# Batch 0 of an attention and feed-forward kernel: transposes back to back, sums a group later, even queries ahead of most feed-forward pieces

## The chip, the cores and the metric

The kernel runs on one core of a Trainium2 chip. A core has a matrix engine (PE, TensorE), VectorE (DVE), ScalarE (ACT), GpSimd (POOL) and SyncE (SP), which run beside each other and wait for one another through semaphores; each works through its own instructions in order. The metric is the device time of one execution in microseconds (us).

## What is computed

Inputs are q, k and v of 8 batches, 12 heads, 448 tokens and 64 numbers per head, and four weight matrices of 768 x 768. The output has 3584 rows of 768.

```
scores = scale * q @ k.T                        # per batch and head
e      = exp(scores - m)                        # m: row maximum
attn   = e / (sum(e) + exp(-m) + 1e-09)
x      = (attn @ v), heads side by side         # [8*448, 768]
h      = max(max(x @ w1, x @ w2), x @ w3)
out    = h @ w_out
```

## The kernel before, in words

Four heads make a group, so each batch has three groups and there are 24 in all. A group's work on PE is: transposing its keys and queries (`transpose_pe` L184 in two halves called pairs, `transpose_once` L214 for the whole group, from group 7 on by a DMA, L229); the scores (`scores` L282), keys times queries, which ACT turns into e by one exponential per score tile (L316) that reads PSUM; the sums (`av`, L524, made of `av_tail` L326 and `av_main` L345), e times the values with a column of ones, divided on DVE by three instructions (L363, L366, L369) into xn; and the transposition of xn into xT (`x_transpose_pe` L389, `x_transpose_all` L404), copied by DVE.

Feed-forward work is cut into pieces: `up_piece` (L427) makes 12 (or 6) matmuls of one weight matrix w[i], i being 0, 1 or 2, and DVE copies the result into hT (L445) or takes the maximum with it (L447); `out_piece` (L452) multiplies hT with w_out. Pieces stand in a list. `fill` (L507) takes pieces off its front while its credit of columns is positive, so PE gets a piece between attention steps. `STEP` (L522) is exactly one piece of two blocks of 192 columns. `share` (L604) spreads what is left over the visits until the next batch is added.

The time at issue is batch 0, groups 0 to 2, before the steady loop at L618. There each group is done in two parts: the odd query blocks "O" (192 columns) first, the even ones "E" (256 columns) later. L546 names the steps: `S01`, `S23` and `S46` are score units, two units to a tile for O and E; `("v", g, p)` is a sum of group g, pair p. The order is written by hand from L547 to L596. Two groups' e buffers exist (`e_buf`, L153).

PSUM comes from two rings: `ps_s` with three buffers (score tiles, sums, and transposes if asked) and `ps_b` with two (transposes, xT and feed-forward results). Asking for a buffer makes its first writer wait for the last reader of the use before. The engine that copies a transposed block out is an argument: DV is DVE, AC is ACT, PL is POOL. `shift_q` (L238) copies queries between partitions for the later groups, on POOL. `prep_v` (L376) puts the values into their buffers, on POOL or DVE.

All inputs are loaded by DMAs that POOL issues, in the order of the program (L142 to L151, then L528 to L533, L553 to L555 and L594 to L596), and converted to 16 bits on the way. A POOL copy that waits for a load, such as `prep_v(1, PL)` at L529, holds back the loads behind it. `warm` (L164) makes matmuls on zeros whose result nobody reads. `make_identity` (L145) makes the matrix that transposes use, on POOL.

Of the kernel before, what the change touches and what calls it, by code (L numbers as in the profile page):

```python
# [16 lines left out]
MMDT = FP16  # L17
# [4 lines left out]
def kernel(  # L22
# [11 lines left out]
    nc = tc.nc  # L34
# [13 lines left out]
    NE, NO = 4 * HP, 3 * HP  # L48
# [17 lines left out]
            name=nc.get_next_instruction_name(),  # L66
# [6 lines left out]
    cpool = ctx.enter_context(tc.tile_pool(name="const", bufs=1))  # L73
# [7 lines left out]
    ps_s = ctx.enter_context(tc.tile_pool(name="ps_s", bufs=3, space=bass.MemoryType.PSUM))  # L81
    ps_b = ctx.enter_context(tc.tile_pool(name="ps_b", bufs=2, space=bass.MemoryType.PSUM))
# [18 lines left out]
    def load_qk(i, names="kq", prs=(0, NP)):  # L101
        b, g = groups[i]
        tiles = raw.setdefault(i, {})
        for nm in names:
            if nm not in tiles:
                t = ld_bufs[nm][i % NL]
                if nm == "q" and i < NF:
                    nc.vector.memset(t[:, 0 : NP * T + 2 : NP * T + 1, :], 0.0)
                tiles[nm] = t
            src = {"q": q, "k": k}[nm][b].rearrange("h s d -> (h s) d")  # L110
            src = src.rearrange("(g r x t) d -> g x r (t d)", g=NG, r=NP, x=P)[g]
            p0, p1 = prs
            nc.gpsimd.dma_start(  # L113
                out=tiles[nm][:, 1 : NP * T + 1].rearrange("x (r t) d -> x r (t d)", r=NP)[:, p0:p1],
                in_=src[:, p0:p1],
            )
# [16 lines left out]
    def load_weight(i, gs=(0, 1, 2)):  # L133
        w = (moe_w1, moe_w2, moe_w3, moe_w_out)[i]
        src = w.rearrange("(g hf p) f -> g p hf f", g=3, hf=2)
        for g in gs:
            nc.gpsimd.dma_start(out=w_sb[i][:, 2 * g : 2 * g + 2, :], in_=src[g])  # L137


    wz = cpool.tile([128, 512], MMDT, name="wz")  # L140
    nc.vector.memset(wz, 0.0)
    load_qk(0, "kq", (0, 1))  # L142
    load_qk(0, "kq", (1, 2))
    ident16 = cpool.tile([128, 128], MMDT, name="ident16")
    make_identity(nc, ident16)  # L145
    load_qk(1, "kq", (0, 1))
    load_qk(1, "kq", (1, 2))
    load_v(0)
# [15 lines left out]
    def warm(n, cols=512):  # L164
        ps = ps_b.tile([128, 512], FP32, tag="b", name="warm")
        for _ in range(n):
            nc.tensor.matmul(
                out=ps[:, 0:cols], lhsT=wz[:, 0:128], rhs=wz[:, 0:cols], start=True, stop=True
            )
# [14 lines left out]
    def transpose_pe(i, pr, pool, k_eng, q_engs):  # L184


        def tile_of():
            if pool is ps_s:
                return ps_s.tile([128, 2, 1024], MMDT, tag="s", name="trT")[:, 0]
            return ps_b.tile([128, 1024], MMDT, tag="b", name="trT")  # L190

        kr, qr = raw[i]["k"], raw[i]["q"]
        kj = (0, 1, 2) if pr == 0 else (3, 4, 5, 6)
        qt = (-1, 1, 3, 5, 0, 2, 4) if pr == 0 else (6, 8, 10, 12, 7, 9, 11, 13)
        n = -(-len(qt) // len(q_engs))
        jobs = [(k_eng, "k", kj[0], kr, [2 * b for b in kj])]
        for e, eng in enumerate(q_engs):
            jobs.append((eng, "q", pr * 7 + e * n, qr, qt[e * n : (e + 1) * n]))
        if i not in KT:
            KT[i] = att_pool.tile([P, T * 128], MMDT, tag="KT", name="KT")  # L200
            QT[i] = att_pool.tile([P, (NB + 1) * 128], MMDT, tag="QT", name="QT")
        tps = [tile_of() for _ in jobs]
        for tp, (eng, nm, o, src, toks) in zip(tps, jobs):
            for j, t in enumerate(toks):
                nc.tensor.transpose(
                    out=tp[:, ts(j, 128)],
                    in_=src[:, t + 1 : t + 3, :].rearrange("x t d -> x (t d)"),
                    identity=ident16,
                )
        for tp, (eng, nm, o, src, toks) in zip(tps, jobs):  # L210
            dst = {"k": KT, "q": QT}[nm][i]
            evac(eng, dst[:, o * 128 : (o + len(toks)) * 128], tp[:, 0 : len(toks) * 128])
# [273 lines left out]
    def add_up(b, q0, qn, order):  # L486
        w = 1 if qn == S else 2
        for i, f0 in order:
            fcs = tuple(range(f0, f0 + w))
            pieces.append((up_piece, (b, fcs, i, q0, qn), NDC * w * (qn + 6)))  # L490
# [16 lines left out]
    def fill(cols):  # L507
        credit[0] += cols
        while pieces and credit[0] > 0:
            f, a, w = pieces.pop(0)  # L510
            f(*a)
            credit[0] -= w
        if not pieces:
            credit[0] = min(credit[0], 0.0)
# [10 lines left out]
        av_tail(i, ej, pr, PW[part])  # L525
        av_main(i, ej, pr, PW[part])

    load_weight(0, (0, 1))  # L528
    prep_v(1, PL)  # L529
    load_weight(0, (2,))  # L530
    prep_v(2, PL)
    load_qk(3)
    load_weight(1)  # L533
# [1 line left out]
    def attend(part, g, *steps):  # L535

        ej = (g + (part == "E") * NG) % NEB
        for st in steps:
            if st[0] == "s":
                for u in st[1:]:  # L540
                    scores(g, ej, u, part)
            else:
                pg, pr = st[1:]
                av(pg, pg % NEB, pr, "O")
# [3 lines left out]
    transpose_pe(0, 0, ps_s, DV, (AC, DV))  # L548
    transpose_pe(0, 1, ps_b, DV, (DV,))
    attend("O", 0, S01, S23, S46)  # L550
    warm(5)
    transpose_pe(1, 0, ps_b, AC, (DV,))
    load_qk(4)  # L553
    load_weight(2)
    load_v(3)  # L555
    attend("O", 1, S01)
    transpose_pe(1, 1, ps_b, AC, (DV,))
    attend("O", 1, S23, S46)
    prep_v(0, DV)
    attend("O", 1, ("v", 0, 0), ("v", 0, 1))  # L560
    transpose_pe(2, 0, ps_b, AC, (DV,))
    attend("O", 2, S01)
    transpose_pe(2, 1, ps_b, DV, (DV,))
    attend("O", 2, ("v", 1, 0), S23)
    x_transpose_pe(0, "O")
    attend("O", 2, S46, ("v", 1, 1), ("v", 2, 0))
    attend("E", 0, S01)
    x_transpose_pe(1, "O")
    attend("E", 0, ("v", 2, 1), S23)
    x_transpose_pe(2, "O")  # L570
    add_up(0, NE, NO, [(i, f) for i in range(3) for f in (0, 2, 4)])
    fill(STEP)
    attend("E", 0, S46)
    fill(STEP)

    for n in (4, 5):
        ej, part, g, pp, pg = n % NEB, "E", n - 3, "E", n - 4
        scores(g, ej, (0, 1), part)
        scores(g, ej, (2, 3), part)
        av(pg, 1 - ej, 0, pp)  # L580
        if n == 4:
            transpose_once(3, "q", AC)
        else:
            x_transpose_pe(0, "E")
        fill(STEP)
        scores(g, ej, (4, 5), part)
        scores(g, ej, (6,), part)
        av(pg, 1 - ej, 1, pp)
        if n == 4:
            transpose_once(3, "k", AC)  # L590
        fill(STEP)
        if n == 4:
            shift_q(3, PL)
            load_v(4)  # L594
            load_qk(5)
            load_weight(3)  # L596
# [21 lines left out]
    for i in range(3, NI):  # L618
        ej, pj = (i + 1) % NEB, i % NEB
        first = i == 3  # L620
        if PE_QK <= i + 2 < NI:
            transpose_dma(i + 2)
        if first:
            load_v(i + 2)
        for vi, units in enumerate(visits):
            n = 3 * i + vi
            scores(i, ej, units)
            if i == 4 and vi == 0:
                prep_v(i, DV)
            if vi < 2:  # L630
                av(i - 1, pj, vi, "E" if first else "EO")
            if vi == 1 and i > 3 * PE_X:
                x_transpose_dma(i - 1)
            if n in adds:
                add_batch(adds[n])
            per = STEP if first and vi < 2 else share(n)
            if vi == 0 and first:
                x_transpose_pe(1, "E")
            if vi == 2 and first:
                x_transpose_pe(i - 1, "E")  # L640
                fill(per / 2)
                prep_v(i, DV)
                add_up(0, 0, NE, [(w, f) for w in range(3) for f in (0, 2, 4)])
                add_out(0)
                per = share(n)
            if vi == 2 and 3 < i <= 3 * PE_X:
                x_transpose_all(i - 1)
            if first:
                fill(per)
                per = 0  # L650
            if i + 1 < PE_QK and vi < 2:
                transpose_once(i + 1, "qk"[vi], (AC, DV)[vi])
            fill(per)
        if i + 1 < PE_QK:
            shift_q(i + 1, nc.gpsimd)
        if first:
            load_qk(i + 3)
        if i < 5:
            load_more(i + 3, i + 4)
        if 5 <= i + 1 < NI:  # L660
            prep_v(i + 1, nc.gpsimd)
        if PE_QK <= i + 2 < NI:
            shift_q(i + 2, nc.gpsimd)
        if i >= 5:
            load_more(i + 3, i + 4)
# [37 lines left out]
```

## Time and profile before

| What | us |
|---|---|
| median of 5 runs (342.68 to 344.95) | 343.85 |
| the profiled execution's own time | 346.1 |
| its span, first to last instruction | 344.3 |
| PE busy | 331.0 |
| DVE busy | 187.0 |
| ACT busy | 151.4 |
| POOL busy | 148.4 |

The profile is of one execution. Busy time adds an engine's instructions up; matmuls overlap, so a busy PE is not one at its peak. The slices cut the span into 40 parts of 8.6 us and give busy shares in tenths. A row of the timeline has the start, the time to the end of the last of its instructions, the engine, line, operation, operands and number, and in brackets how long the engine stood before it and which instruction ended that wait. A row of a table of windows has the stretch, its length, then busy time and number of instructions of PE, PE's weight loads, DVE, ACT and POOL, then the granted clock of PE as a share of full speed, the mean busy share of the DMA engines, and GB/s.

### The profile page before, as it was taken

The page shows a single profiled execution, that of the slowest core. Times are in us where ns is not written, and L with a number is a line of the kernel's source. Part 1 is how long each engine was busy: PE and PEld are TensorE (multiplying, and loading weights), DVE is VectorE, ACT ScalarE, POOL GpSimd, SP SyncE. Part 2 cuts the span into 40 slices and gives each one's busy share as a digit, 9 for nine tenths or more (in the row PEclk, how much of TensorE's full clock was granted, in tenths as well). Part 3 has the DMA queues.
Part 4 walks back from the last instruction along what each step waited for, and adds up shares of the span by engine and source line. Part 5 has one row for each costly group of instructions (what it writes and reads, how often), then busy time and mean ns, then how long its engine had stood idle before and what let it go on. Part 6 is the DMA issues. An engine that isn't in the chain of part 4 may idle for free.

```text
span 344.3 us, 9827 instructions
## 1 busy us (share of the span) xinstructions
PE 331.0 (96%) x4175; PEld 200.4 (58%) x4175; DVE 187.0 (54%) x407; ACT 151.4 (44%) x181; POOL 148.4 (43%) x265
## 2 busy tenths in 40 slices
PE   7789899999999999999999999999999999999994
PEld 3567688765556555556555655556555655565552
DVE  3464556555465556556556556556556555565552
ACT  2758657664554444444444444444444444200000
POOL 8596477594580729272565246272553000000000
PEclk9999989999999999999999999999999999999999
DMA  7999999799999899979977999999970450123006
GB/s 101 178 183 203 203 206 170 101 156 200 160 116 104 155 230 167 110 127 211 186 108 76 142 242 110 170 95 166 218 129 9 124 125 3 30 71 100 0 19 165
DMA packets 84844, 46.19 MB, mean 134 GB/s; under 512 B 53312, under 2 KB 81344, under 8 KB 84800
## 3 DMA queue, kind: packets, MB, share of 16 engines
q0 software_dynamic: 29440, 22.03, 48.6%
q1 hardware_dynamic: 55120, 23.37, 39.9%
q8 instruction: 32, 0.52, 0.6%
q10 hardware_dynamic: 240, 0.16, 0.2%
q14 instruction: 12, 0.10, 0.1%
HBM read 44.04 MB, written 11.01 MB: 160 GB/s over the span
## 4 chain that ended last, share of the span: by engine, by line
PE 87%; DMA 6%; POOL 5%; issue 1%; DVE 0%; POOLq 0%
PE p_i L436 46%; PE op_ps L460 16%; PE avp L353 11%; PE stp L296 10%; DMA w<-in_moe_w_dram 4%; DMA ld_v<-in_v_dram 2%; PE avp L336 2%; POOL ld_q L113 1%; POOL ld_k L113 1%; POOL w L137 1%; PE trT L221 1%; PE xtp L409 0%; POOL vx L379 0%; POOL ld_v L123 0%; POOL ld_v L126 0%
## 5 line engine op out<-in xcount | busy, mean ns | idle before, releaser
L316 ACT ACTIVATE e<-stp 128x896 f16<-128x896 f32 (+4 forms) x171 | 144.2, 903 | 139.0 <-PE stp L296 138.9
L436 PE MATMUL p_i<-xT,w 128*128 128x448 f16 (+2 forms) x972 | 174.9, 333 | 2.5 <-DMA w<-in_moe_w_dram 2.2
L436 PEld LDWEIGHTS <-w 128*128 128x128 f16 x972 | 90.6, 98 | 70.7 <-issue 5.1
L241 POOL COPY QT<-QT 64x384 f16<-64x384 f16 (+1 forms) x84 | 46.8, 557 | 96.6 <-DMA QT<-ld_q 61.7
L447 DVE TENSOR_TENSOR hT<-hT,p_i 128x448 f16<-128x448 f16 (+2 forms) x96 | 59.6, 621 | 48.9 <-PE p_i L436 48.7
L460 PE MATMUL op_ps<-w,hT 128*128 128x384 f16 (+2 forms) x342 | 58.1, 323 | 0.0
L296 PE MATMUL stp<-QT,KT 64*64 64x448 f16 (+2 forms) x756 | 47.9, 340 | 2.6 <-DVE QT L182 2.0
L353 PE MATMUL avp<-vx,e 128*128 128x65 f16 x1152 | 45.7, 194 | 0.0
L460 PEld LDWEIGHTS <-hT 128*128 128x128 f16 x342 | 32.1, 98 | 22.7 <-issue 2.0
L467 DVE TENSOR_SCALAR o_sb<-op_ps 128x384 f32<-128x384 f32 (+2 forms) x57 | 31.2, 549 | 24.3 <-PE op_ps L460 22.6
L445 DVE CAST hT<-p_i 128x448 f16<-128x448 f32 (+2 forms) x48 | 30.0, 625 | 22.4 <-PE p_i L436 22.3
L353 PEld LDWEIGHTS <-e 128*128 128x128 f16 x1152 | 39.0, 98 | 2.3
L369 DVE TENSOR_TENSOR xn<-avp,rb 128x512 f16<-128x512 f32 (+1 forms) x54 | 34.1, 632 | 1.9
L296 PEld LDWEIGHTS <-KT 64*64 64x64 f16 x756 | 15.7, 105 | 26.7 <-issue 23.0
L363 DVE TENSOR_SCALAR rb<-avp 128x8 f32<-128x8 f32 (+1 forms) x54 | 8.9, 165 | 40.7 <-PE avp L353 40.6
L379 POOL COPY vx<-ld_v 128x768 f16<-128x768 f16 x21 | 17.2, 819 | 9.0 <-issue 4.8
L336 PEld LDWEIGHTS <-e 64*64 64x64 f16 x768 | 15.0, 108 | 8.1 <-issue 1.7
L113 POOL DMA_DIRECT2D ld_q<-in_q_dram x26 | 18.6, 714 | 2.1 <-DMA w<-in_moe_w_dram 1.2
L113 POOL DMA_DIRECT2D ld_k<-in_k_dram x26 | 18.4, 708 | 2.2 <-DMA w<-in_moe_w_out_dram 1.1
L336 PE MATMUL avp<-vt,e 64*64 64x65 f16 x768 | 15.5, 193 | 0.8 <-ACT e L316 0.7
L126 POOL DMA_DIRECT2D ld_v<-in_v_dram x24 | 15.4, 641 | 1.5 <-DMA w<-in_moe_w_dram 1.3
L123 POOL DMA_DIRECT2D ld_v<-in_v_dram x24 | 15.2, 634 | 1.7 <-DMA w<-in_moe_w_dram 1.7
(41 smaller groups left out, 87.3 us busy)
## 6 DMA issues: line engine op xcount, KB each, us to landing
out_dram<-o_sb SPq DMA_DIRECT2D x54, 192.0 KB, 4.3
ld_v<-in_v_dram POOLq DMA_DIRECT2D x48, 128.0 KB, 4.4
ld_k<-in_k_dram POOLq DMA_DIRECT2D x22, 224.0 KB, 6.9
ld_q<-in_q_dram POOLq DMA_DIRECT2D x22, 224.0 KB, 7.6
w<-in_moe_w_dram POOLq DMA_DIRECT2D x9, 384.0 KB, 9.3
w<-in_moe_w_out_dram POOLq DMA_DIRECT2D x3, 384.0 KB, 8.5
ld_k<-in_k_dram POOLq DMA_DIRECT2D x4, 112.0 KB, 3.7
ld_q<-in_q_dram POOLq DMA_DIRECT2D x4, 112.0 KB, 4.0
```

Of the source, the lines that this page charges most:

```text
L113: nc.gpsimd.dma_start(out=tiles[nm][:, 1 : NP * T + 1].rearrange("x (r t) d -> x r (t d)", r=NP)[:, p0:p1], in_=src[:, p0:p1],)
L241: eng.tensor_copy(out=t[d0 : d0 + HP, o * 128 : (o + n) * 128], in_=t[s0 : s0 + HP, a * 128 : (a + n) * 128],)
L296: nc.tensor.matmul(out=stp[half * HP : half * HP + HP, par, j * qn : (j + 1) * qn], lhsT=k_block(i, pr, h2, x[half]), rhs=q_cols(i, pr, h2 ...
L316: nc.scalar.activation(out=dst, in_=src, func=AF.Exp, scale=scale)
L336: nc.tensor.matmul(out=ps[half * HP : half * HP + HP, hh, j * D1 : (j + 1) * D1], lhsT=eF[hh * HP : hh * HP + HP, o : o + HP], rhs=vt[hh * ...
L353: nc.tensor.matmul(out=ps[:, hh, j * D1 : (j + 1) * D1], lhsT=eF[:, o : o + 128], rhs=vx[:, 2 * pr + hh, (x[0]), 0:D1], start=False, stop= ...
L369: nc.vector.tensor_tensor(out=xn[i][:, pr, ws[0] : ws[0] + nw].rearrange("p j h d -> p h j d"), in0=acc[:, :, :, 0:D], in1=rb[:, :, 0:nw]. ...
L436: nc.tensor.matmul(out=p_i[:, j * qn : (j + 1) * qn], lhsT=w_sb[i][:, dc, ts(fc, 128)], rhs=xT[b][:, dc, q0 : q0 + qn], start=(dc == 0), s ...
L445: nc.vector.tensor_copy(out=dst, in_=src)
L447: nc.vector.tensor_tensor(out=dst, in0=dst, in1=src, op=ALU.max)
L460: nc.tensor.matmul(out=op_ps[:, 0:w], lhsT=hT[bp][:, fc, ts(t, 128)], rhs=wout_sb[:, fc, c : c + w], start=(fc == 0), stop=(fc == NFC - 1),)
L467: nc.vector.tensor_scalar(out=o_sb[:, c : c + w], in0=op_ps[:, 0:w], scalar1=1.0 / LAMBDA, scalar2=None, op0=ALU.mult,)
```

## The change

It does the following, all in batch 0. The identity's memset goes from POOL to DVE, ahead of the loads. All three parts of the first weight matrix are issued before POOL's `prep_v(1)`. Three warm matmuls stand where five stood. Group 1's second pair is transposed straight after its first, in `ps_s`; group 2's too, with the keys copied by ACT. Group 0's second sum stands after group 2's transposes, and group 1's first sum after all of group 2's odd scores. Of the feed-forward pieces of the odd columns only those of weights 0 and 1 are listed at first; three calls of `fill` are taken out, so five pieces stand ahead of the last visit of group 3 (L625, third round) where eight stood. The three pieces of weight 2 for the odd columns are listed later, behind the even columns of weights 0 and 1. Group 3's transposes are copied by DVE instead of ACT.

```diff
--- before.py
+++ after.py
@@ -139,10 +139,11 @@
 
     wz = cpool.tile([128, 512], MMDT, name="wz")
     nc.vector.memset(wz, 0.0)
+    ident16 = cpool.tile([128, 128], MMDT, name="ident16")
+    nc.vector.memset(ident16, 0.0)
     load_qk(0, "kq", (0, 1))
     load_qk(0, "kq", (1, 2))
-    ident16 = cpool.tile([128, 128], MMDT, name="ident16")
-    make_identity(nc, ident16)
+    make_identity(nc, ident16, nomemset=True)
     load_qk(1, "kq", (0, 1))
     load_qk(1, "kq", (1, 2))
     load_v(0)
@@ -525,9 +526,8 @@
         av_tail(i, ej, pr, PW[part])
         av_main(i, ej, pr, PW[part])
 
-    load_weight(0, (0, 1))
+    load_weight(0)
     prep_v(1, PL)
-    load_weight(0, (2,))
     prep_v(2, PL)
     load_qk(3)
     load_weight(1)
@@ -548,30 +548,27 @@
     transpose_pe(0, 0, ps_s, DV, (AC, DV))
     transpose_pe(0, 1, ps_b, DV, (DV,))
     attend("O", 0, S01, S23, S46)
-    warm(5)
+    warm(3)
     transpose_pe(1, 0, ps_b, AC, (DV,))
+    transpose_pe(1, 1, ps_s, AC, (DV,))
     load_qk(4)
     load_weight(2)
     load_v(3)
-    attend("O", 1, S01)
-    transpose_pe(1, 1, ps_b, AC, (DV,))
-    attend("O", 1, S23, S46)
+    attend("O", 1, S01, S23, S46)
     prep_v(0, DV)
-    attend("O", 1, ("v", 0, 0), ("v", 0, 1))
+    attend("O", 1, ("v", 0, 0))
     transpose_pe(2, 0, ps_b, AC, (DV,))
-    attend("O", 2, S01)
-    transpose_pe(2, 1, ps_b, DV, (DV,))
-    attend("O", 2, ("v", 1, 0), S23)
+    transpose_pe(2, 1, ps_b, AC, (DV,))
+    attend("O", 2, ("v", 0, 1), S01, S23, S46, ("v", 1, 0))
     x_transpose_pe(0, "O")
-    attend("O", 2, S46, ("v", 1, 1), ("v", 2, 0))
+    attend("O", 2, ("v", 1, 1), ("v", 2, 0))
     attend("E", 0, S01)
     x_transpose_pe(1, "O")
     attend("E", 0, ("v", 2, 1), S23)
     x_transpose_pe(2, "O")
-    add_up(0, NE, NO, [(i, f) for i in range(3) for f in (0, 2, 4)])
+    add_up(0, NE, NO, [(i, f) for i in range(2) for f in (0, 2, 4)])
     fill(STEP)
     attend("E", 0, S46)
-    fill(STEP)
 
     for n in (4, 5):
         ej, part, g, pp, pg = n % NEB, "E", n - 3, "E", n - 4
@@ -579,15 +576,14 @@
         scores(g, ej, (2, 3), part)
         av(pg, 1 - ej, 0, pp)
         if n == 4:
-            transpose_once(3, "q", AC)
+            transpose_once(3, "q", DV)
         else:
             x_transpose_pe(0, "E")
-        fill(STEP)
         scores(g, ej, (4, 5), part)
         scores(g, ej, (6,), part)
         av(pg, 1 - ej, 1, pp)
         if n == 4:
-            transpose_once(3, "k", AC)
+            transpose_once(3, "k", DV)
         fill(STEP)
         if n == 4:
             shift_q(3, PL)
@@ -640,7 +636,8 @@
                 x_transpose_pe(i - 1, "E")
                 fill(per / 2)
                 prep_v(i, DV)
-                add_up(0, 0, NE, [(w, f) for w in range(3) for f in (0, 2, 4)])
+                for w, cols in ((0, (0, NE)), (1, (0, NE)), (2, (NE, NO)), (2, (0, NE))):
+                    add_up(0, *cols, [(w, f) for f in (0, 2, 4)])
                 add_out(0)
                 per = share(n)
             if vi == 2 and 3 < i <= 3 * PE_X:
```

## Prediction

> **What bounds the kernel now.** I read the page first (busy time, slices), then the waits of the matrix engine (PE), then its timeline, then single microseconds around its longest wait.
>
> ```profile
> span 344.3 us, 9827 instructions
> ...
> PE 331.0 (96%) x4175; PEld 200.4 (58%) x4175; DVE 187.0 (54%) x407; ACT 151.4 (44%) x181; POOL 148.4 (43%) x265
> ...
> PE   7789899999999999999999999999999999999994
> ```
>
> PE is busy for 96% of the span, and from the sixth slice (43 us) on it never falls below nine tenths. Whatever happens before is a late start of that continuous stretch. So the end moves by what changes in PE's waits, or in its rate, before the stretch; moved PE work alone moves nothing.
>
> ```profile
> PE p_i L436 <- DMA w<-in_moe_w_dram: 2.2, 2, 1.5
> PE stp L296 <- DVE QT L182: 2.0, 3, 0.9
> PE warm L167 <- DVE wz L141: 1.2, 1, 1.2
> PE avp L336 <- ACT e L316: 0.7, 1, 0.7
> ```
>
> These are PE's largest waits over the whole span. Two are for weights (w2 and w3 of the reference, index 1 and 2 in the code): 0.7 and 1.5 us. Three are for transposed queries being copied out. The timeline of PE places them:
>
> ```profile
> 11.59 0.36 PE L296 MATMUL stp<-QT,KT 64*64 64x192 f16 x8 [0.71 <-DVE QT L182]
> ...
> 17.61 0.36 PE L296 MATMUL stp<-QT,KT 64*64 64x192 f16 x8 [0.94 <-DVE QT L182]
> ...
> 32.51 0.83 PE L436 MATMUL p_i<-xT,w 128*128 128x192 f16 x8 [0.70 <-DMA w<-in_moe_w_dram]
> ...
> 41.05 0.83 PE L436 MATMUL p_i<-xT,w 128*128 128x192 f16 x8 [1.49 <-DMA w<-in_moe_w_dram]
> ...
> 43.75 2.11 PE L436 MATMUL p_i<-xT,w 128*128 128x192 f16 x12
> ```
>
> The last row is a piece of 12 matmuls that takes 2.11 us; the same piece took 1.15 at 34.51. The single microseconds say why (the number after the engines is the granted clock):
>
> ```profile
> 40.00:41.00 1.00, 0.00 (x0) 0.00 (x0) 0.00 (x0) 0.00 (x0) 0.16 (x1) 1.00 1.43 194
> ...
> 42.00:43.00 1.00, 1.00 (x21) 0.60 (x18) 0.48 (x1) 0.69 (x1) 0.92 (x2) 0.69 1.30 204
> 43.00:44.00 1.00, 1.00 (x26) 0.93 (x19) 0.02 (x1) 1.00 (x3) 0.90 (x2) 0.50 1.27 206
> 44.00:45.00 1.00, 1.00 (x8) 0.95 (x7) 0.74 (x3) 0.85 (x2) 0.90 (x3) 0.50 1.22 221
> 45.00:46.00 1.00, 1.00 (x12) 0.96 (x10) 0.10 (x1) 0.00 (x0) 0.94 (x2) 0.61 1.13 200
> ```
>
> PE stands from 39.42 to 41.05 (1.63 us), and then the clock falls to half for about 3.4 us. That loses 0.31+0.50+0.50+0.39 = 1.7 us. The DMA share is above 1 throughout: transfers land in the order issued, back to back (the last part of index 1 at 32.46, of index 2 at 41.0, the values of group 3 at 42.43), so the weights can't come sooner.
>
> **The change, part by part.** I walk both orders of instructions with durations of this trace: seven transposes 0.39 us from start to start, a 192-column piece 1.08, the exponential of 1024 columns 0.93 (0.50 for 512), normalising chain on VectorE (DVE) 0.19+0.21+0.36, 0.05 from engine to engine. Walked so, the order before reaches its first 256-column piece at 46.65 without the clock's fall; 46.65+1.7 = 48.3, and the trace has 48.2.
>
> *Start to the first feed-forward piece.* Two warm matmuls fewer: 2 x 0.215 = 0.43 us. Group 1's transposes run together from 9.7 to 10.9, while the copies (ACT 0.38+0.48, DVE 0.62+0.68) overlap them; the first sums start at 13.2 instead of 14.67. But group 2's queries land at 14.97; before, PE reached them at 16.11 without waiting, now it waits 1.0 at 14.0. Then its last query tile needs a PSUM buffer that ACT's key copy frees (0.7), the scores another (0.5), the sums of group 1 another (0.4). So the lead is spent on a transfer and on buffers: the first piece starts at 24.1 instead of 24.59 in the trace and 24.7 in the walk. I take -0.6, between 0 and -1.4.
>
> The identity's memset moves from POOL (0.26) to DVE, where it lies before three memsets of 0.11 and ahead of nothing urgent (DVE idles until 5.51). POOL issues the four loads of group 1 some 0.2 earlier; they land paced by the queue, not by their issue. The third part of the first weight is issued before the values of group 1 are awaited (about 13.7, not 17.65), but it follows the same transfers in the queue. I take 0 for both; bounds +0.1 and -0.3. SP's queue has nothing before 59 us.
>
> *Even queries, 24 to 43 us.* Before: 48.2-24.6 = 23.6 us, of which 0.70+1.63 wait for weights, 1.7 is the half clock and 0.2 a wait for xT: 19.4 of work. Now three pieces (3 x 1.08 = 3.24) come later, so 16.1 of work. No piece of index 1 comes before 37 us or of index 2 before 55: all landed, both waits go. The half clock goes with its idle time. That removes 4.0.
>
> What is late next? Consecutive score tiles. Half a group's scores are two tiles, ps_s has three buffers, and the sums take one too. Without a piece between, four score tiles follow one another, and the fourth must wait until ACT has done the first. One even group costs ACT 3 x 0.93 + 0.50 = 3.3 us, which the row of four exponentials shows nearly dense:
>
> ```profile
> 26.41 3.49 ACT L316 ACTIVATE e<-stp 128x1024 f16<-128x1024 f32 x4 [1.46 <-PE stp L296]
> ```
>
> PE's own work for an even group with one piece is about 4.0, with two 5.1. ACT is thus not the bound on average, but it is in bursts. The walk gives waits of 0.93 and 0.27 at 26 to 27.5, 0.62 at 28.7, 0.23 and 0.69 at 32.8 to 34, 0.14 at 38: +2.9. From below: 1.3, if hand-offs hide; from above 3.9, if each burst costs a whole tile more. The nearest row (exponentials back to back) is the walk's, so 2.9. The copies of group 3's transposes move from ACT (0.92, 0.96) to DVE (0.62 each); they would add 0.24 on ACT, and queue on DVE behind a chain of 0.8, with POOL's shift behind them: scores of group 3 start 3 us after it, hidden. Their inputs landed at 24.68 and 25.77, needed at 28; group 4's by 34.68, needed at 38.2. prep_v of group 3 stands on DVE at about 43.4, its values land at 42.43: 1 us of cover. If that were gone, the two pieces behind it would hold both ps_b buffers.
>
> *The three pieces given back.* The share per visit grows from 5553 to 6266 columns, so one more piece falls into some visits. Twice a second piece follows a transpose while DVE still copies, with two ps_b buffers: 0.2+0.4 = +0.6, bounds 0 and 0.6.
>
> *Sum* (the three pieces go out of one stage and into the next, 3.24 each way): -0.6 -0.7 -1.63 -1.7 +2.9 +0.6 = -1.1 us. Span 344.3-1.1 = 343.2; the profiled execution's own time 346.1 (1.8 lie around the span) would become 345.0. The median 343.85 is 2.25 below that execution, so I subtract 1.1 from it: 342.7.
>
> [...]
>
> **Rivals.**
> *A, the half clock moves to the front (slower).* Between 12.6 and 16.2 the new order waits 0.58+0.99+0.66, some 1.7 us idle in 3.4 after matmul tails, in a stretch of transposes. Before, the clock held at 1.07 idle (11.7 to 15.1: 0.42 and 0.65) and fell at 1.63: the point that decides lies between. Price 1.7: -1.1+1.7 = +0.6, 344.4; where bursts also cost their upper bound, +1.6, 345.5. Against: PE isn't the bound there, so part hides.
> *B, the score bursts cost their lower bound.* 1.3 instead of 2.9: -2.7, 341.1. For it: hand-offs without 0.05 each make the walk 1 us shorter.
> *C, the gain isn't in typical runs.* If the half clock belongs to the profiled execution only ([...] they spread by 2.3 us), 1.7 of the gain is missing: +0.6, 344.4. The order then only exchanges weight waits for score waits.
>
> **How the numbers follow.** The sum as it stands 0.42 (own range 341.7 to 343.7), B 0.18, C 0.25, A 0.15. Half a per cent is 1.7 us, about what a measurement can tell from no change: faster means below 342.1, slower above 345.6. B and a quarter of the first case are faster: 0.30. A with dear bursts, and A with C together, are slower: 0.13. The rest, 0.57, is within. The range reaches from B, 340.9, to A's upper end, 345.6.
>
> **What would show it.** After: no wait of p_i for weights; granted clock 1.0 from 39 to 46 us; new waits of stp for ACT's e between 26 and 35, some 2.9 in sum; a wait for ld_q near 14; first 256-column piece near 43. Wrong, if the clock is below 1 near 16 to 20 (A), if the score waits are near 1 (B), if prep_v of group 3 waits for its values, or if weights land later than now.

## The result and the profile after

| | before | after |
|---|---|---|
| median of all runs, us | 343.51 (71 runs) | 343.61 (36 runs) |
| profiled execution, us | 346.1 | 344.58 |
| its span, us | 344.3 | 342.8 |

The ratio of the times is 1.0009, with a 95% interval from 0.9997 to 1.0022: no difference of a size that matters, +0.3 us by the ratio and between -0.1 and +0.8. Yet the two profiled spans differ by 1.5 us in favour of the change. That contradiction is what the experiments had to settle. The ratio leaves out one execution of the changed kernel, of 348.59 us, as more than 1.5% above its fastest.

The page of the profile after, the same rows as before:

```profile
span 342.8 us, 9819 instructions
...
PE 330.2 (96%) x4173; PEld 199.3 (58%) x4173; DVE 189.0 (55%) x409; ACT 149.9 (44%) x180; POOL 148.3 (43%) x264
...
PE   7887999999999999999999999999999999999994
```

PE reaches nine tenths in the fifth slice now, not in the sixth. Its waits over the whole span after:

```profile
PE stp L297 <- ACT e L317: 1.5, 3, 0.8
...
PE p_i L437 <- DVE o_sb L468: 0.8, 1, 0.8
PE stp L297 <- DVE xn L370: 0.7, 2, 0.5
...
PE p_i L437 <- DVE KT L183: 0.4, 1, 0.4
...
PE p_i L437 <- DMA w<-in_moe_w_dram: 0.3, 1, 0.3
```

The waits for the second and third weights are gone; score tiles (stp) that wait for ACT's exponentials stand first instead. The 0.3 us for a weight is the third part of the first one. The timeline of PE after places them:

```profile
24.62 0.83 PE L437 MATMUL p_i<-xT,w 128*128 128x192 f16 x8 [0.33 <-DMA w<-in_moe_w_dram]
...
26.92 0.41 PE L297 MATMUL stp<-QT,KT 64*64 64x256 f16 x8 [0.80 <-ACT e L317]
...
29.08 0.30 PE L297 MATMUL stp<-QT,KT 64*64 64x256 f16 x4 [0.20 <-DVE xn L370]
...
32.90 0.41 PE L297 MATMUL stp<-QT,KT 64*64 64x256 f16 x8 [0.20 <-ACT e L317]
...
33.81 0.30 PE L297 MATMUL stp<-QT,KT 64*64 64x256 f16 x4 [0.50 <-ACT e L317]
...
41.78 3.77 PE L437 MATMUL p_i<-xT,w 128*128 128x192 f16 x36
...
50.45 2.99 PE L437 MATMUL p_i<-xT,w 128*128 128x256 f16 x24
...
63.08 1.47 PE L437 MATMUL p_i<-xT,w 128*128 128x256 f16 x12 [0.37 <-DVE KT L183]
...
65.63 2.78 PE L437 MATMUL p_i<-xT,w 128*128 128x256 f16 x24
...
69.74 1.14 PE L461 MATMUL op_ps<-w,hT 128*128 128x384 f16 x6
```

The first out_piece starts at 69.74 us; before it started at 71.53. From there to the last instruction ten of the 13 profiled executions of this text took between 271.95 and 272.26 us, so the start of the first out_piece tells how an order did. (Before took 272.8 and after 273.0; the latter has a wait of 0.84 us at 121.9.) In the single microseconds after, PE stays full and the granted clock stays at 1.00 where it had fallen:

```profile
40.00:41.00 1.00, 1.00 (x18) 0.90 (x19) 0.84 (x2) 1.00 (x2) 0.10 (x1) 1.00 1.43 195
...
43.00:44.00 1.00, 1.00 (x12) 0.90 (x10) 1.00 (x3) 0.89 (x2) 0.96 (x2) 1.00 1.19 196
```

So the profiled execution of before lost 1.7 us to half clock in this stage and that of after lost none. Without that difference the two would be level at the first out_piece (71.53-1.7 = 69.83 against 69.74).

### The profile page after: what moved, and what is told of

Read it like the earlier page. It is cut to its first block, busy times and chain, and to the rows that moved or that the text cites. A ratio compares the mean times of both kernels' runs of the same rounds, so it can differ in the third digit from the quotient of the medians.

```text
span 342.8 us, 9819 instructions
## 1 busy us (share of the span) xinstructions
PE 330.2 (96%) x4173; PEld 199.3 (58%) x4173; DVE 189.0 (55%) x409; ACT 149.9 (44%) x180; POOL 148.3 (43%) x264
## 4 chain that ended last, share of the span: by engine, by line
PE 89%; DMA 5%; POOL 2%; DVE 1%; issue 1%; ACT 1%; POOLq 0%
PE p_i L437 48%; PE op_ps L461 16%; PE avp L354 11%; PE stp L297 11%; DMA w<-in_moe_w_dram 3%; PE avp L337 2%; DMA ld_k<-in_k_dram 2%; ACT e L317 1%; POOL ld_q L113 1%; PE trT L222 1%; POOL ld_k L113 1%; PE xtp L410 0%; DVE KT L183 0%; DVE xn L370 0%; DVE o_sb L468 0%
```

## The theories

**Theory 1** (rival C of the prediction): the half clock after the weight wait belongs to few executions. In the others the change exchanges waits for weights for waits for score buffers, and the sum is near zero. **Theory 2** (the sum on record): the half clock is in typical runs, its removal is worth 1.7 us, and something that shows only later took it back. **Rival A**: a half clock at the front takes its place. The parts of the change (loads, transposes, feed-forward pieces) might also pull in opposite directions.

## The experiments

**The kernel before again (b0).** No edit.

> The kernel before, unchanged, to see the granted clock of each of its runs. Theory 1 (the half clock after the weight wait belongs to few executions): most runs have a mean clock of 0.996 or more, as the runs of the changed kernel have, and runs with 0.993 are over 1 us longer than the others. Theory 2 (the half clock is in typical runs, and something later took its gain away): most runs have 0.994 or less. Ratio 1.00 by both.

Ratio 1.000 (0.998 to 1.002), median 343.41. Of its 22 executions 19 have a mean granted clock of 0.996 or more, as theory 1 wants. The other three, 0.992, 0.993 and 0.995, took 344.81, 346.99 and 347.92 us. In the 176 further executions of before that were measured beside the kernels below, four have 0.995 or less. So the half clock is rare. The profiled execution is one of the rare ones: it has the half clock again, with a longer wait (timeline, then single microseconds of PE):

```profile
40.61 1.40 PE L436 MATMUL p_i<-xT,w 128*128 128x192 f16 x8 [1.71 <-DMA w<-in_moe_w_dram]
```

```profile
41.00:42.00 1.00, 1.00 (x9) 0.95 (x7) 0.00 (x0) 0.00 (x0) 1.00 (x2) 0.50 1.33 202
42.00:43.00 1.00, 1.00 (x12) 0.68 (x13) 0.56 (x1) 0.20 (x1) 1.00 (x3) 0.50 1.26 202
```

It took 344.81 us, 1.4 above its median, as that of before (346.1) took 2.6 above. Why both profiled executions of before are of the rare kind is not known.

**The third weight's wait taken away (b1).** The three odd-column pieces of the third weight read the second weight, so the third matrix is left out of that part of the maximum.

```diff
-                    lhsT=w_sb[i][:, dc, ts(fc, 128)],
+                    lhsT=w_sb[1 if (b, i, q0) == (0, 2, NE) else i][:, dc, ts(fc, 128)],
```

> The kernel before, but the three odd-column pieces of the third weight in batch 0 read the second weight's tile, which has landed (so the third matrix is left out of that part of the maximum). PE's 1.6 us wait at 39.4 goes. Theory 1: about -1.6 us (0.995), since the half clock was rare. Theory 2: about -3.3 us (0.990).

Ratio 0.9968 (0.9950 to 0.9986), -1.1 us: nearer to theory 1 (-1.6) than to theory 2 (-3.3), which its interval (-0.5 to -1.7) excludes.

**The half clock alone (d1).** Six matmuls on zeros fill the wait; the wait stays.

```diff
+            if first and vi == 0:
+                warm(6)
             if first:
                 fill(per)
```

> The kernel before with six matmuls on zeros (1.3 us) just ahead of the third weight's first piece, so that PE isn't idle during that wait; the wait itself stays. It prices the half clock alone. If the half clock is rare in the runs: 0 to +0.2 us (1.000). If it is in all: -1.7 us (0.995). In half of them: -0.8 us (0.9977).

Ratio 1.0015 (0.9991 to 1.0038). The profile shows the edit at work: the matmuls on zeros at 38.51, the weight piece right behind, full clock after.

```profile
38.51 1.46 PE L167 MATMUL warm<-wz 128*128 128x512 f16 x6
39.80 1.35 PE L436 MATMUL p_i<-xT,w 128*128 128x192 f16 x12
```

```profile
42.00:43.00 1.00, 1.00 (x31) 0.97 (x20) 0.34 (x2) 1.00 (x2) 0.84 (x2) 1.00 1.29 204
```

Keeping the clock up gains nothing that shows: -0.3 us at most by the interval, where theory 2 wanted -1.7. The added matmuls end at 39.97, ahead of this landing at 40.27, and cost this execution nothing.

**The feed-forward part alone** (b2), on the kernel before (fills out, the third weight's odd pieces later):

```diff
-    add_up(0, NE, NO, [(i, f) for i in range(3) for f in (0, 2, 4)])
+    add_up(0, NE, NO, [(i, f) for i in range(2) for f in (0, 2, 4)])
...
-    fill(STEP)
...
-        fill(STEP)
         scores(g, ej, (4, 5), part)
...
-                add_up(0, 0, NE, [(w, f) for w in range(3) for f in (0, 2, 4)])
+                for w, cols in ((0, (0, NE)), (1, (0, NE)), (2, (NE, NO)), (2, (0, NE))):
+                    add_up(0, *cols, [(w, f) for f in (0, 2, 4)])
```

> The kernel before with only the feed-forward part of the change: three fills out, the third weight's odd pieces listed later. By the walk, waits for weights (0.7 and 1.6) go, waits for score buffers of 3.1 and later 0.6 come: +1.2 us (1.0035) without a half clock in the kernel before (theory 1), -0.5 us (0.9985) with it (theory 2).

Ratio 1.0027 (1.0015 to 1.0040), +0.9 us: theory 1's side. This part costs time. Its timeline has the waits of the changed kernel 0.7 to 1.0 us later, and one of them is longer (0.50 at 33.86, where the changed kernel has 0.20 at 32.90):

```profile
27.59 0.41 PE L296 MATMUL stp<-QT,KT 64*64 64x256 f16 x8 [0.80 <-ACT e L316]
...
33.86 0.41 PE L296 MATMUL stp<-QT,KT 64*64 64x256 f16 x8 [0.50 <-ACT e L316]
34.78 0.30 PE L296 MATMUL stp<-QT,KT 64*64 64x256 f16 x4 [0.50 <-ACT e L316]
```

**The feed-forward part undone** (b3) in the changed kernel; the edit is the one above reversed.

> The changed kernel with the feed-forward part undone: transposes back to back, sums later, loads and identity as changed, eight pieces ahead. By the walk the lead of 0.6 us at 24 us is lost in a longer wait for the second weight (1.2 in place of 0.6), and the wait for the third weight stays: 0.0 us (1.000) by both theories. A rival, that the transposes gain outright because weights land earlier with the earlier issue: -0.6 us (0.998).

Ratio 0.9972 (0.9954 to 0.9990), -1.0 us. My walk had said 0: this was a miss. Both weight waits are there in its profile, 1.03 and 1.19 us, and no half clock follows:

```profile
32.13 0.83 PE L437 MATMUL p_i<-xT,w 128*128 128x192 f16 x8 [1.03 <-DMA w<-in_moe_w_dram]
...
40.05 0.83 PE L437 MATMUL p_i<-xT,w 128*128 128x192 f16 x8 [1.19 <-DMA w<-in_moe_w_dram]
```

**The same with the old loads** (b4): identity on POOL and the first weight's third part behind `prep_v(1, PL)`, as before.

```diff
-    ident16 = cpool.tile([128, 128], MMDT, name="ident16")
-    nc.vector.memset(ident16, 0.0)
     load_qk(0, "kq", (0, 1))
     load_qk(0, "kq", (1, 2))
-    make_identity(nc, ident16, nomemset=True)
+    ident16 = cpool.tile([128, 128], MMDT, name="ident16")
+    make_identity(nc, ident16)
...
-    load_weight(0)
+    load_weight(0, (0, 1))
     prep_v(1, PL)
+    load_weight(0, (2,))
```

> The transpose part alone (b3) with the old order of loads and the identity wholly on POOL, so only transposes, sums, warm matmuls and the engine of group 3's copies are changed. If the -1 us of b3 comes from loads that land earlier: 0.0 us (1.000). If it comes from the order of transposes, whose lead moves idle time from the third weight's wait to the second's (1.0 and 1.2 us in place of 0.4 to 0.7 and 1.6 to 2.0) so that neither drops the clock: -0.9 us (0.9975).

Ratio 1.0003 (0.9984 to 1.0022). So the transposes and sums alone gain nothing here, and the gain of the last kernel came with the loads.

**The loads alone** (e4), on the kernel before: the edit above reversed.

> The kernel before with only the identity's memset on DVE and the first weight's third part issued before the values of group 1 are awaited. If the 1 us between b3 and b4 comes from the loads: the third weight lands about 0.5 us earlier and this gains 0.5 to 1 us (0.997 to 0.9985). If that was scatter of landings between executions: 1.000.

Ratio 0.9979 (0.9967 to 0.9992), -0.7 us. The loads gain. In its profiled execution the third weight's wait ends at 39.67, the earliest of all:

```profile
39.67 0.83 PE L437 MATMUL p_i<-xT,w 128*128 128x192 f16 x8 [1.22 <-DMA w<-in_moe_w_dram]
...
68.58 2.11 PE L461 MATMUL op_ps<-w,hT 128*128 128x384 f16 x12
```

Over all profiled executions the third weight lands on average at 40.35 us with the old loads (seven: 39.75 to 41.00) and at 40.05 with the new ones (six: 39.62 to 40.62). That is 0.3 of the 0.7 us, with as much scatter; the rest is not shown.

**The changed kernel again (a0).**

> The changed kernel, unchanged, on the same chip as these. Ratio to before 1.001. Its first profile has PE waits of 0.84 us at 121.9 us for DVE's o_sb: if they belong to the changed kernel's order they come again, if they are chance of that execution they don't.

Ratio 1.0004 (0.9987 to 1.0021). Its profile has no wait for o_sb at 121.9, and a span of 341.8 us: that wait was chance. The waits for score buffers are the same to 0.1 us.

**Pieces at the score bursts (c1).** The changed kernel with three fills moved, so that the first weight's pieces stand between the bursts.

```diff
     attend("E", 0, S46)
+    fill(STEP)
...
             transpose_once(3, "q", DV)
+            fill(STEP)
...
             transpose_once(3, "k", DV)
-        fill(STEP)
+        else:
+            fill(STEP)
```

> The changed kernel with its six early pieces placed again: one more fill after the last even scores of group 0, one after group 3's queries are transposed, and none after its keys, so the first weight's pieces stand between the bursts of score tiles and the second weight's come after 33 us. If the waits for score buffers are what gave the removed weight waits back, they shrink from about 2.9 to about 1.2 us by the walk: -1.6 us against the changed kernel, -1.2 us (0.9965) against the kernel before. If those waits only hid other lateness (DMA landings), 0 against the changed kernel (1.000).

Ratio 0.9968 (0.9949 to 0.9986), -1.1 us against the kernel before; the changed kernel in the same series had 1.0004, so -1.2 against that (0.9968/1.0004 = 0.9964). Here a version beats both kernels. The waits for score buffers were the price: one of them is left in its timeline, and from its first piece to its first 256-column piece it takes 17.46 us (25.02 to 42.48), where the changed kernel's repeat takes 18.75 (23.88 to 42.63).

```profile
34.50 0.30 PE L297 MATMUL stp<-QT,KT 64*64 64x256 f16 x4 [0.50 <-ACT e L317]
...
42.48 3.02 PE L437 MATMUL p_i<-xT,w 128*128 128x256 f16 x24
```

Its profiled execution shows rival A besides: matmuls on half clock from 15 to 18.3 us, after waits for keys and queries of 0.8 and 0.7 us. From its single microseconds:

```profile
14.00:15.00 1.00, 0.43 (x9) 0.26 (x6) 0.77 (x3) 0.73 (x2) 0.59 (x1) 0.95 1.43 193
15.00:16.00 1.00, 1.00 (x11) 0.87 (x9) 0.35 (x1) 0.00 (x0) 0.00 (x0) 0.50 1.45 205
```

**The same with more warm matmuls** (e1), against that early half clock.

```diff
-    warm(3)
+    warm(5)
...
     attend("O", 1, ("v", 0, 0))
+    warm(4)
```

> c1 with five warm matmuls again ahead of group 1's transposes and four (0.86 us) in front of group 2's, where PE waits for queries that land near 14.6 us. The profiles of c1 and of b4 had half clock from 15 to 18.4 us, those of the changed kernel and b3 had not. If that early half clock is frequent in c1's runs and costs the 1.1 us by which c1's first piece was late, this is 0.5 to 1 us faster than c1: 0.994 to the kernel before. If it is rare or the waits hide it: as c1, 0.997, or 0.4 us worse for the added matmuls, 0.998.

Ratio 0.9988 (0.9974 to 1.0002): not faster than the last kernel, and measured on another chip, so the difference between the two is not settled. Its profiled execution has full clock throughout and starts its first out_piece at 68.44, 0.8 us ahead of the last kernel's 69.26. So the early half clock may have cost that one execution about 0.8. None of the 22 executions of this kernel has a mean clock of 0.995 or less, where six of the last kernel's 22 have: the added matmuls do keep the clock up. What they cost beside that is not settled.

**The pieces moved, old transposes and loads (e6).**

> c1's placing of the feed-forward pieces (three of the third weight late, six at the bursts and after 33 us) with the transposes, sums and loads of the kernel before. By the walk, with no weight wait left to absorb it, the earlier start is worth 1.1 us: this kernel -0.1 us against the kernel before (1.000), c1 -1.2 (0.9965). If the placing alone does it: 0.9965 here too.

The edit is that of the pieces at the score bursts, on the kernel with the feed-forward part alone. Ratio 0.9996 (0.9984 to 1.0007): -0.1 us, the number that the walk gave, but not for the walk's reason alone. Beside c1 this kernel also lets ACT, not DVE, copy group 3's transposes. Its ACT has these copies among the exponentials:

```profile
29.74 0.93 ACT L180 ACTIVATE QT<-trT 128x896 f16<-128x896 f16 x1
...
31.92 0.96 ACT L180 ACTIVATE KT<-trT 128x896 f16<-128x896 f16 x1
```

where c1 has six exponentials in one row:

```profile
30.92 4.94 ACT L317 ACTIVATE e<-stp 128x1024 f16<-128x1024 f32 x6 [0.59 <-PE stp L297]
```

From the first piece to the first 256-column piece it takes 18.19 us, against 17.46 in c1 and in e1. Of the 1.1 us between the first out_pieces of e6 (69.53) and e1 (68.44) 0.73 thus arise there, next to ACT's copies, and only 0.35 are an earlier start (24.55 against 24.20). No run changes the copies alone. And c1 was measured on another chip; on this one e1, with the new transposes, has 0.9988. So what the transposes and loads are worth without a weight wait comes to 1.0 us beside c1 and to 0.3 beside e1, and is not settled. With the wait there (b4) the transposes were worth nothing.

## Why the prediction was right and where it was off

The measured median lies in the range, and no measurable change was the likeliest class. But the central 342.7 is 0.9 us too low, and the class came out by rival C, which had a chance of 0.25, and not by the sum, which had 0.42. By its steps:

**Start to the first piece (-0.6).** It began at 23.80 us, not 24.1; before 24.59. The lead was spent where described: on queries of group 2, on a PSUM buffer, and on score waits. But the queries landed at 14.54, not 14.97, and the wait for them was 0.28 us, not 1.0. Right, and 0.2 larger.

**Waits for weights (-0.7 and -1.6).** Both gone. But the 1.63 belongs to a landing at 41.00, the latest of the seven profiled executions with the old loads; at their mean, 40.35, there was 0.65 less to gain. A wait of 0.33 for the first weight's third part, which landed at 24.57, was not foreseen; in the repeat it landed at 23.17 and there was none.

**Waits for score buffers (+2.9).** From the first piece to the first 256-column piece the prediction has 16.1 us of work and 2.9 of waits, 19.0. The trace has 23.80 to 42.77 (41.78 plus one piece of 0.99): 18.97, the 0.33 for the weight included. The waits stand where they were placed, but as listed they come to 1.5 us for ACT and 0.2 for xn, nearer to rival B's 1.3 than to 2.9. A listed wait can fall short of its cost (that of the third weight is listed as 1.49 and was counted as 1.63), but not by that much. So the length of the stage was right, in part by luck: it divides into work and waits otherwise than was said.

**Given back later (+0.6).** 0.37 us for KT at 63.08, and 0.21 in the two pieces at 50.45, which took 2.99 where such a pair takes 2.78 (at 65.63). Together 0.6: right.

**The half clock (-1.7).** This is the step that failed, and not in the trace: there it went, as said. What failed was the sentence that subtracts the whole sum, 1.7 of half clock included, from the median of the runs. The profiled execution of before was 2.25 us above that median, and I read this as a constant offset. It was largely the half clock itself (1.55 us by the table below), and 0.8 us more came after the first out_piece.

The clocks of the runs show how rare it is. In the 13 profiled executions those with a half clock ahead of the last 3 us have a mean clock of 0.992 or 0.993, the others 0.996 to 1.000; one stretch of it, 3.41 us in 343, takes 0.005 off the mean. So 0.995 or less tells of at least one. Of 198 timed executions of before 7 have a mean of 0.995 or less. Their median is 345.3 us, that of the other 191 is 343.46. So the median of before held no 1.7 us that the change could take away. That is rival C. Its reason, a period that the runs need not share, fits what the two profiles show. The clock of before falls to half at 42.37 us and again at 342.74, 300.37 us later, which is 88 times 3.4133; that of after falls only at 340.80. In steps of 3.4133 us from the first instruction on, both falls of before stand 1.41 us into a step, that of after 2.88.

What the half clock costs follows from the kernels that keep the third weight's wait. The start of their first out_piece is set by its landing:

| kernel | third weight lands | first out_piece | difference | clock after the wait |
|---|---|---|---|---|
| before | 41.00 | 71.53 | 30.53 | half |
| before again | 40.56 | 71.05 | 30.49 | half |
| feed-forward part undone | 40.01 | 68.96 | 28.95 | full |
| the same, old loads | 40.57 | 69.53 | 28.96 | full |
| warm in the wait | 40.27 | 69.22 | 28.95 | full |
| loads alone | 39.62 | 68.58 | 28.96 | full |

So in these six executions everything ahead of the landing is absorbed, and the half clock is worth 1.55 us. With the mean landing of the seven profiled executions with the old loads, 40.35, the kernel before at full clock starts its first out_piece at 69.3; the changed kernel starts it at 69.74 and 69.59, 0.3 to 0.4 later. Among timed executions with a clock above 0.995 the two are level within 0.2: 343.46 before, 343.35 and 343.61 in the two series of the changed kernel. So rival C was right in kind, and its +0.6 was too much.

**Rival A** was right too, for part of the runs. Of the 36 executions of the changed kernel 11 have a mean clock of 0.995 or less, and their median is 345.02 us against 343.35 for the other 25. With a0 it is 14 of 50, against 7 of 198 before. It goes with the moved transposes and two warm matmuls fewer:

| kernels | executions | clock 0.995 or less |
|---|---|---|
| transposes moved, three warm matmuls (after, a0, b3, b4, c1) | 108 | 29 |
| transposes as before (before, b0, b1, b2, d1, e4, e6) | 291 | 9 |
| transposes moved, five and four warm matmuls (e1) | 22 | 0 |

(On e1's chip before has 2 of 51.) In the profiled executions of b4 and c1 the half clock stands at 15 to 18.5 us; where it stands in the timed ones was not seen. So the change takes a half clock out of few executions and puts one into more of them, and that, more than the order at full clock, makes the +0.3. Where the wait for the third weight stays, it absorbs this as well: the six such executions of b4 have a median of 343.78, the other eight 343.71.

**The parts:** loads -0.7, transposes 0.0 (absorbed by the weight wait), feed-forward +0.9. Their sum is +0.2, and +0.3 was measured. That they add up so well is in part luck: each has an interval of some 0.4 us or more to either side, and a part's worth hangs on the others (loads on top of the transposes, b4 to b3, gave -1.0). The prediction put the loads at 0, between +0.1 and -0.3; that term was 0.7 off, though the interval of the run (-0.3 to -1.1) touches its bound. It did not see that the feed-forward part alone loses, and it did not price the transposes where the weight wait stays.

## What to carry to other kernels

Before a stall's price is taken off a median, ask whether the profiled execution is a typical one: if its time lies well above the runs (here 346.1 us against a median of 343.51), its rarest feature (here a stretch of half clock) may be just what sets it apart, and the mean clock of each run can tell (0.995 or less in 7 of 198). The wait for the third weight absorbed every gain ahead of it (28.95 or 28.96 us from the landing to the first out_piece in four kernels), so judge an early gain by whether such a wait follows. And work put between bursts that share few buffers is not filler: with it taken out the bursts waited (b2, +0.9 us), so move a late piece by putting in its place another whose data have landed (c1, 1.2 us less than the changed kernel).

## What was not expected of the hardware

A stretch of half clock lasted 3.41 us each time (before, b0, b4, c1; in before from 42.37 to 45.78). In the 3.41 us ahead of the fall PE had stood for 1.63 us in before, 2.09 in b0, 1.41 in b4 and 1.12 in c1. The clock held through 1.30 us from 23.36 to 26.78 in after, through 1.21 in such a stretch around e4's weight wait, and through 1.41 from 14.04 to 17.45 in before (which the steps of that profile divide at 15.06). So idle time in these stretches, as far as they can be placed, does not sort them, and the point between 1.07 and 1.63 us that rival A counts on is not shown. In b4 and c1 transposes stand around the fall (from 13.76 to 17.48 and from 13.87 to 17.33 us); no run isolates whether they have a part in it. One and the same load landed between 39.62 and 41.00 us in 13 profiled executions, which by the table of landings moves the end of the kernel as much as the whole change could.
